# Top-k attention and highway layer on one core: a copy, two list rounds, warm matmuls and the end's products change places

## The chip, the cores and the metric

The kernel runs on one core of a Trainium2 chip. The core's engines work side by side, each on its own instructions in their order: TensorE (PE: matmuls and transposes; its weight loads are listed as PEld), VectorE (DVE), ScalarE (ACT), GpSimd (POOL), and SyncE (SP), which here issues DMAs. The metric is the device time of one execution in microseconds, as the median of several runs.

## The reference

For 8 batches of 8 heads, with 576 positions and head size 64, each query keeps the scores that are no smaller than its 32nd largest, takes a softmax over them and averages the values. The result goes, position by position, through a highway layer of width 512:

```python
scores = scale * np.matmul(q, k.transpose(0, 1, 3, 2))
kth = np.partition(scores, -top_k, axis=-1)[..., -top_k:-top_k + 1]   # top_k = 32
scores = np.where(scores >= kth, scores, -1000000000.0)
attn = softmax(scores)
x = np.matmul(attn, v)      # then to (4608, 512)
H = np.maximum(x @ w_h, 0.0)
T = 1.0 / (1.0 + np.exp(-(x @ w_t + b_t)))
return (T * H + (1.0 - T) * x)
```

(softmax is written out in the original.)

## The kernel before

**Tiling.** A group is 128 queries of one batch, for all 8 heads; queries are dealt to four groups per batch by their index modulo 4, and the 64 left over at the end of a batch share a group with those of the next batch. A group is worked through in pairs of tiles: one pair is two tiles of 128 queries by 576 keys. There are 144 pairs, numbered n, and the main loop (line 1016) makes one step for each.

**What happens to a pair.** `scores` (line 222) multiplies queries by keys on PE into a score bank in PSUM, of which there is one (`bigps`, bufs=1, line 99). `evac` (line 244) has ACT copy it with a Relu into SBUF, as z (zfirst for pair 0). `tree` (line 255) lets DVE take the maximum of the two halves of each row; for all pairs but the first two it reads one half from the score bank itself, so the bank is free again only when tree is done. `folds` (line 275) fold twice more on DVE, into hi, hh and h3 with widths 288, 144 and 72; POOL restores the smaller values by integer subtraction and addition (`minima`, line 298; pair 0's are done on DVE). `lists` (line 386) then draws sorted lists of eight from these with DVE's MAX8 and MATCH_REPLACE, and `lists_rest` merges them into the 32nd largest. ACT makes a penalty from it (pen), PE transposes score and penalty together, ACT takes the exponential (et), and `values` (line 1012, through `av`) multiplies it with the values; ACT copies this sum out as xs. When a group is complete, its rows are normed and go through the highway layer (`ffn_x`, `ffn_h`, `ffn_t`, `ffn_e`, `ffn_o`).

**The order of the work.** Instructions of PE, DVE, ACT and POOL are issued through a wrapper (`Pinned`, line 28) that keeps each engine's instructions in the order of the program, so the order written out by hand is the order on each engine, and line 38 is the line of nearly every instruction in the profile. The lists are Python generators, each of whose steps issues one instruction: `run(gens, rounds)` (line 411) takes so many steps of each list in turn. From step 3 on, unfinished lists are handed to `folds` as `fill`, which puts them between operations that depend on each other.

**The opening.** `turn_first` (line 144) transposes queries of the first tile: first for heads 0 and 1 (h0 = 0), then for the others (h0 = 1), and copies them into kq; on DVE in both cases. `turn` (line 175) transposes keys (kin 0, 1, 2, 3) and has ACT copy them. After its scores, step n puts WARM[n] matmuls without use on PE (`spin`, line 960), so that its clock stays granted: 9, 7 and 8 in steps 1, 2 and 3. In steps 0 and 1 `run(opening, 1)` takes one round of the pair's lists behind its folds; the rest follows in step 2, and what is left there is the fill of step 3.

**The end.** Behind the loop (from line 1114) the last pairs and the last two groups are written out by hand: gp, the last but one, and gl, the last. For gl, `final_norm` (DVE: a reciprocal and a product), `final_turn` (PE transpose, copy to xT on DVE, a half on POOL), `final_h` and `final_t` (PE products) are done in blocks of 128 columns as soon as heads are ready, so that little is left behind the last values. For gp, `ffn_gate` is a tanh on ACT, `ffn_e` a product on DVE over 512 columns (x <- t, x), `ffn_o` another one (d <- x, d) and an output transfer on SP's queue. `ffn_d(gl)` (d <- hps, xh) and `final_o` (two products on each half, and a transfer for each) end the program. `judge` turns the tests for a slower exact path into a flag.

Of the kernel before, what the change touches and what calls it, by code (L numbers as in the profile page):

```python
# [21 lines left out]
NZ = 3  # L22
NPEN = 3
IDLE = {11: 3, 10: 8, 9: 3, 3: 3, 2: 3}
WARM = {1: 9, 2: 7, 3: 8}


class Pinned:
# [42 lines left out]
class Ops:  # L71
# [72 lines left out]
    def turn_first(self, pr, h0, h1):  # L144


        nc, P = self.nc, self.P
        kqps = self.ztps.tile([P, 512], FP32, tag="zt", name="kqps")
        for hp in range(h0, h1):
            nc.tensor.transpose(  # L150
                kqps[:, hp * P : (hp + 1) * P],
                pr["qc"][:, 2 * hp : 2 * hp + 2, :].rearrange("p h d -> p (h d)"),
                self.ident[:],
            )
        nc.vector.tensor_copy(
            pr["kq"][:, 1, h0:h1, 0:P],
            kqps[:, h0 * P : h1 * P].rearrange("p (h q) -> p h q", q=P),
        )
# [644 lines left out]
def kernel(  # L803
# [10 lines left out]
    nc = tc.nc  # L814
# [60 lines left out]
    with ExitStack() as cm:  # L875
        ops = Ops(cm, tc, shared, exact=False)

        def load_weights():
            for src, dst in ((moe_w_h, wh), (moe_w_t, wt)):
                ops.nc.gpsimd.dma_start(  # L880
                    dst[:], src.rearrange("(g p) n -> p g n", p=P)
                )
            bt_bcast = bass.AP(
                tensor=moe_b_t.tensor, offset=moe_b_t.offset, ap=[[0, P], [1, dm]]
            )
            ops.nc.gpsimd.dma_start(bt[:], bt_bcast)
# [7 lines left out]
        def out_rows(g):  # L894
            if not g.rem:
                r0 = g.b * S + g.qt
                return [out[r0 : r0 + JP : J, :]]
            ends = [(g.b + i) * S for i in (0, 1)]
            return [out[r1 - R : r1, :] for r1 in ends]
# [48 lines left out]
        def have(n):  # L948
            return 0 <= n < NPR
# [10 lines left out]
        def spin(n, warm=None):  # L960
            if n and warm is None:
                warm = ops.fps.tile([P, 512], FP32, tag="fp", name="warm")
            for _ in range(n):
                ops.nc.tensor.matmul(
                    warm[:], idle[:, 0:P], idle[:], start=True, stop=True
                )
# [44 lines left out]
        late, fill, opening = [], [], []  # L1011
        def values(m):
            g, pi = pairs[m]
            ops.av(m, g, pi, preps[g.b]["vb"])

        while step <= NPR:
            n = step
            if have(n):
                ops.tree(n)
                if n < 2:  # L1020
                    ops.minima(n, ops.folds(n, *pairs[n], []))
                    opening += ops.lists(n, *pairs[n])
                    ops.run(opening, 1)
                elif n % 2:
                    nq = n // 2 + 1
                    ops.minima(nq, ops.folds(nq, *pairs[n - 1], fill))
                    fill = []
                if NHP <= n + 1 < 2 * NHP:
                    ops.turn(pr, "qin", n + 1 - NHP, None, 1)
                if n == NHP:  # L1030
                    ops.load(pr, "qin", 3, None, None, 1)
                if n == 2 * NHP:
                    ops.turn_rest(pr, 0, NHP, ("qrest",))
            if n == 5:
                load_weights()
            if have(n - 4):
                ops.mask(n - 4, *pairs[n - 4], tis=(0,))
            kind = fg = None
            nextg = None
            if ffn and (ffn[0][0] != "x" or n % 2):  # L1040
                kind, fg = ffn.pop(0)
                if kind == "t" and ffn and ffn[0][0] == "x":
                    nextg = ffn.pop(0)[1]
            if have(n - 5):
                spin(2 * (NPR - n < 12))
                values(n - 5)
            if have(n - 4):
                ops.mask(n - 4, *pairs[n - 4], tis=(1,))
            if have(n + 1):
                g, pi = pairs[n + 1]  # L1050
                spin(IDLE.get(NPR - n, 0))
                ops.scores(n + 1, g, pi, preps[g.b])
                ops.evac(n + 1)
                if n + 2 < NHP:
                    ops.turn(pr, "kin", n + 2, True)
            if n in WARM:
                spin(WARM[n], ops.ztps.tile([P, 512], FP32, tag="zt", name="warm"))
            if kind == "x":
                ops.ffn_x(fg)
            if kind == "h":  # L1060
                ops.ffn_h(fg)
                ops.ffn_r(fg)
                ops.ffn_d(fg)
            if nextg:
                ops.ffn_x(nextg)
            if kind == "t":
                ops.ffn_t(fg)
                if n < NPR - 1:
                    ops.ffn_e(fg)
                    ops.ffn_o(fg, *out_rows(fg))  # L1070
            if n == 3:
                ops.values_rest(pr)
                ops.values(pr, 0)
            if n == 4:
                ops.values(pr, 1)
            ended = False
            if have(n - 5):
                g, pi = pairs[n - 5]
                ended = pi == len(g.pairs) - 1 and (not g.rem or g.r0 > 0)
            if n % 2:  # L1080
                gens = ops.lists_rest(n // 2 - 1, *pairs[n - 3]) if have(n - 3) else []
                late = gens[2:]
                gens = gens[0:2]
                ops.run(gens)
                ops.run(late, 2)
            else:
                ops.run(late)
                if n == 2:
                    gens = opening
                else:  # L1090
                    gens = ops.lists(n - 2, *pairs[n - 2]) if have(n - 2) else []
                ops.run(gens, 2 * (n > 2))
                if ended:
                    ops.norm(pairs[n - 5][0])
                ops.run(gens, 3)
                if have(n + 1):
                    gens, fill = gens[0:2], gens[2:4]
                ops.run(gens)
            if have(n - 4):
                ops.trans(n - 4)  # L1100
            if ended and not pairs[n - 5][0].quick:
                ops.norm_heads(pairs[n - 5][0])
            for piece in pieces.pop(n, []):
                piece()
            if n % 2 == 0 and have(n - 3):
                g, pi = pairs[n - 3]
                if pi == len(g.pairs) - 1:
                    ops.settle(g)
            if ended:
                g = pairs[n - 5][0]  # L1110
                ffn += [("x", g), ("h", g), ("t", g)]
            step += 1
# [43 lines left out]
        part(1)  # L1156
        values(m + 1)
        ops.final_norm(gl, 2, 3)
        ops.ffn_gate(gp)
        ops.ffn_e(gp)  # L1160
        gl.ps = ops.fps.tile([P, 512], FP32, tag="fp", name="hps")
        ops.final_h(gl, 0, 2)
        values(m + 2)
        ops.final_turn(
            gl, 2, 3, ops.ztps.tile([P, 512], FP32, tag="zt", name="xtps")
        )
        ops.final_norm(gl, 3, 4)
        ops.final_t(gl, 0, 2)
        judge(banks[3])
        ops.final_turn(  # L1170
            gl, 3, 4, ops.ztps.tile([P, 512], FP32, tag="zt", name="xtps")
        )
        ops.ffn_o(gp, *out_rows(gp))
        ops.final_h(gl, 2, 3)
        ops.final_t(gl, 2, 3)
# [6 lines left out]
    with tc.If(taken > 0):  # L1182
        with tc.For_i(0, B, 1) as b:
            with ExitStack() as cm:
                ops = Ops(cm, tc, shared, exact=True)
# [17 lines left out]
                n = 0  # L1203
# [51 lines left out]
```

## Time and profile before

| | |
|---|---|
| median of 5 runs | 830.69 us (830.54 to 830.89) |
| profiled execution | 830.62 us |
| its span, first to last instruction | 828.9 us |
| mean granted TensorE clock | 0.989 |
| DVE busy | 814.1 us, 98% of the span |
| ACT busy | 760.4 us, 92% |
| POOL busy | 710.4 us, 86% |
| PE busy | 708.2 us, 85% |

All times in the profile are microseconds from the span's start. In a timeline row stand the start, the length, the engine, the line, the operation, what it writes and reads (`out<-in` by the program's names), its shape, and how often it follows itself; a bracket gives the idle time of the engine just before it, and what ended it. A row can stand for several equal instructions. Lengths of neighbours on one engine can overlap, so the cost of an instruction in a full queue is the distance from its start to the next one's.

### The profile page before, as it was taken

How to read it: one execution, taken by the hardware profiler on the slowest of the kernel's cores; microseconds unless marked ns; L12 is line 12 of the kernel's file. 1: busy time of each engine (PE TensorE's matmuls, PEld its weight loads, DVE VectorE, ACT ScalarE, POOL GpSimd, SP SyncE). 2: the span in 40 equal slices, each digit the busy share in tenths (PEclk: the TensorE clock that was granted, in tenths of full speed). 3: DMA queues.
4: the chain of work that ended last, by engine and by line, in shares of the span. 5: the costliest groups of instructions: out<-in, count | busy, mean ns of one | idle time of the engine just before them, and what ended most of it. 6: DMA issues, size and time to landing. Idle time of an engine off the chain costs nothing.

```text
span 828.9 us, 20198 instructions
## 1 busy us (share of the span) xinstructions
PE 708.2 (85%) x6582; PEld 490.0 (59%) x6635; DVE 814.1 (98%) x4173; ACT 760.4 (92%) x1522; POOL 710.4 (86%) x460
## 2 busy tenths in 40 slices
PE   8788888888888888888888898878988888899986
PEld 4565566565566556665566565656556655665654
DVE  5999999999999999999999999999999999999997
ACT  4899999899999999899999999989999999988985
POOL 5888888798889889978889988888888989887993
PEclk9999999999999999999999999999999999999999
DMA  8564233234254441433325342323413321211222
GB/s 183 136 109 84 65 90 75 59 68 88 40 101 85 78 90 30 75 71 65 90 53 92 70 93 61 64 53 71 110 32 65 52 40 40 40 35 26 45 39 56
DMA packets 105329, 58.40 MB, mean 70 GB/s; under 512 B 82304, under 2 KB 91904, under 8 KB 105216
## 3 DMA queue, kind: packets, MB, share of 16 engines
q1 hardware_dynamic: 93200, 37.47, 17.7%
q0 software_dynamic: 11200, 19.27, 16.4%
q8 instruction: 54, 0.88, 0.5%
q14 instruction: 59, 0.48, 0.2%
q10 hardware_dynamic: 816, 0.30, 0.1%
HBM read 30.67 MB, written 18.35 MB: 59 GB/s over the span
## 4 chain that ended last, share of the span: by engine, by line
DVE 94%; PE 3%; ACT 1%; POOL 1%; issue 0%; POOLq 0%; DVEq 0%
DVE w L38 53%; DVE m L38 20%; DVE hi L38 11%; DVE hh L38 6%; DVE h L38 3%; PE warm L38 1%; PE ps L38 1%; PE zt L38 1%; PE t L38 1%; DVE scales L38 0%; POOL hh L38 0%; ACT pen L38 0%; POOL hi L38 0%; ACT z L38 0%; ACT kq L38 0%
## 5 line engine op out<-in xcount | busy, mean ns | idle before, releaser
L38 PE MATMUL ps<-kq 64*128 64x64 f32 (+3 forms) x1280 | 202.9, 440 | 45.1 <-DVE hi L38 39.5
L38 ACT ACTIVATE pen<-z,m 128x576 bf16<-128x576 f32 x286 | 225.6, 790 | 1.2 <-DVE m L38 1.0
L38 PE MATMUL zt<-ident,z 128*128 128x128 f32 x1140 | 212.9, 280 | 2.0 <-ACT xT L38 2.0
L38 PE MATMUL zt<-nident,pen 128*128 128x128 bf16 x1148 | 205.5, 220 | 0.0
L38 ACT ACTIVATE z<-ps 128x1152 f32<-128x1152 f32 x143 | 161.8, 1131 | 43.6 <-PE ps L38 40.9
L38 POOL TENSOR_TENSOR hi<-z,hi 128x1152 int32<-128x1152 int32 (+1 forms) x72 | 188.2, 2613 | 11.2 <-DVE hh L38 5.6
L38 POOL TENSOR_TENSOR hi<-hi,z 128x1152 int32<-128x1152 int32 (+1 forms) x72 | 189.1, 2627 | 5.6
L38 PEld LDWEIGHTS ps<-kq 64*128 64x128 f32 (+1 forms) x1280 | 103.2, 177 | 140.9 <-issue 80.2
L38 PEld LDWEIGHTS zt<-ident,z 128*128 128x128 f32 x1140 | 161.3, 141 | 16.6 <-ACT xT L38 2.9
L38 ACT ACTIVATE et<-zt 128x512 bf16<-128x512 f32 x287 | 162.0, 601 | 5.6 <-PE zt L38 1.8
L38 POOL TENSOR_TENSOR hh<-hi,hh 128x576 int32<-128x576 int32 x71 | 104.5, 1471 | 70.9 <-DVE w L38 70.9
L38 PEld LDWEIGHTS <-pen 128*128 128x128 bf16 x1440 | 152.0, 106 | 16.1 <-ACT pen L38 10.7
L38 DVE MAX8 m<-w 128x8 f32<-128x168 f32 x576 | 158.8, 315 | 0.0
L38 PE MATMUL zr<-v,et 128*128 128x65 bf16 (+1 forms) x1590 | 98.1, 196 | 44.6 <-ACT et L38 37.3
L38 PEld LDWEIGHTS <-et 128*128 128x128 bf16 (+1 forms) x1600 | 69.1, 101 | 85.3 <-ACT et L38 82.4
L38 DVE MAX8 w<-hi 128x8 f32<-128x288 f32 x288 | 115.6, 440 | 0.0
L38 POOL TENSOR_TENSOR hh<-hh,hi 128x576 int32<-128x576 int32 x71 | 100.3, 1412 | 5.6
L38 DVE TENSOR_TENSOR hi<-ps,z 128x576 f32<-128x576 f32 x142 | 104.3, 734 | 0.5 <-ACT z L38 0.5
L38 DVE MAX8 w<-hh 128x8 f32<-128x72 f32 x576 | 96.4, 217 | 0.0
L38 DVE MATCH_REPLACE8 w<-m,w 128x168 f32<-128x168 f32 x288 | 88.6, 313 | 0.0
L38 PE MATMUL zr<-ident,z 128*128 128x128 f32 x284 | 67.3, 290 | 8.0 <-ACT xs L38 7.9
L38 ACT ACTIVATE x<-xs,scales 128x64 f32<-128x64 f32 x272 | 68.2, 336 | 0.0
(106 smaller groups left out, 1182.3 us busy)
## 6 DMA issues: line engine op xcount, KB each, us to landing
x<-d POOLq DMA_DIRECT2D x35, 256.0 KB, 3.8
vin<-in_v_dram SPq DMA_DIRECT2D x8, 1024.0 KB, 5.5
kin<-in_k_dram SPq DMA_DIRECT2D x63, 128.0 KB, 3.3
out_dram<-d SPq DMA_DIRECT2D x31, 256.0 KB, 2.3
out_dram<-t POOLq DMA_DIRECT2D x30, 256.0 KB, 4.2
qin<-in_q_dram SPq DMA_DIRECT2D x56, 128.0 KB, 3.0
qrest<-in_q_dram SPq DMA_DIRECT2D x8, 128.0 KB, 3.5
vrest<-in_v_dram SPq DMA_DIRECT2D x8, 128.0 KB, 3.1
```

The costliest lines, as they stand in the source:

```text
L38: return self._tc.keep_in_program_order(fn(*args, **kw))
```

## The change

Four edits. The copy of the other heads' queries of the first tile (h0 = 1) goes from DVE to ACT, where it stands behind the evacuation of pair 0 and ahead of the copy of kin 1. Pair 0's lists take three rounds in step 0 instead of one, so two MATCH_REPLACE and two MAX8 more stand ahead of pair 1's tree, and lists are finished in step 2, with nothing left as fill for step 3. Step 1 issues 5 warm matmuls instead of 9. At the end, gp's gate (ACT) goes behind the copy of the last values; gp's `ffn_e` (DVE) goes from behind the third block's norm to behind the last block's turn, just ahead of `ffn_o`; the last block's norm goes ahead of the third block's turn.

```diff
-WARM = {1: 9, 2: 7, 3: 8}
+WARM = {1: 5, 2: 7, 3: 8}
...
-        nc.vector.tensor_copy(
+        copy = nc.scalar.copy if h0 else nc.vector.tensor_copy
+        copy(
             pr["kq"][:, 1, h0:h1, 0:P],
             kqps[:, h0 * P : h1 * P].rearrange("p (h q) -> p h q", q=P),
         )
...
                     opening += ops.lists(n, *pairs[n])
-                    ops.run(opening, 1)
+                    ops.run(opening, 1 + 2 * (n == 0))
...
         values(m + 1)
         ops.final_norm(gl, 2, 3)
-        ops.ffn_gate(gp)
-        ops.ffn_e(gp)
         gl.ps = ops.fps.tile([P, 512], FP32, tag="fp", name="hps")
         ops.final_h(gl, 0, 2)
         values(m + 2)
+        ops.ffn_gate(gp)
+        ops.final_norm(gl, 3, 4)
         ops.final_turn(
             gl, 2, 3, ops.ztps.tile([P, 512], FP32, tag="zt", name="xtps")
         )
-        ops.final_norm(gl, 3, 4)
         ops.final_t(gl, 0, 2)
         judge(banks[3])
         ops.final_turn(
             gl, 3, 4, ops.ztps.tile([P, 512], FP32, tag="zt", name="xtps")
         )
+        ops.ffn_e(gp)
         ops.ffn_o(gp, *out_rows(gp))
```

## The prediction

> **What bounds the kernel now.** I read four views: busy time and the chain of waits on the page, then the timeline of the first 25 us and of the last 12 us, where the edits lie. From the page, engine shares and the engines of the chain that ended last:
>
> ```profile
> PE 708.2 (85%) x6582; PEld 490.0 (59%) x6635; DVE 814.1 (98%) x4173; ACT 760.4 (92%) x1522; POOL 710.4 (86%) x460
> ...
> DVE 94%; PE 3%; ACT 1%; POOL 1%; issue 0%; POOLq 0%; DVEq 0%
> ```
>
> VectorE (DVE) is the bound. From 22 to 800 us its waits add up to one of 0.4 us, so only its start, its stalls in the opening and its idle time at the end can change; the 780 us between are untouched. The timeline of the opening, all engines (start, length, engine, line, operation, in brackets the idle time before it and what ended it):
>
> ```profile
> 7.66 1.14 ACT L38 ACTIVATE zfirst<-ps 128x1152 f32<-128x1152 f32 x1 [1.28 <-PE ps L38]
> ...
> 8.12 0.56 DVE L38 COPY kq<-kqps 128x384 f32<-128x384 f32 x1 [2.01 <-PE kqps L38]
> ...
> 8.82 0.76 DVE L38 TENSOR_TENSOR hi<-zfirst 128x576 f32<-128x576 f32 x1
> ...
> 14.04 2.10 PE L38 MATMUL warm<-idle 128*128 128x512 bf16 x8
> ...
> 15.01 0.74 DVE L38 TENSOR_TENSOR hi<-ps,z 128x576 f32<-128x576 f32 x1
> ...
> 16.07 1.30 PE L38 MATMUL ps<-kq 64*128 64x512 f32 x8
> ...
> 17.42 1.13 ACT L38 ACTIVATE z<-ps 128x1152 f32<-128x1152 f32 x1 [2.15 <-PE ps L38]
> ...
> 18.58 0.76 DVE L38 TENSOR_TENSOR hi<-ps,z 128x576 f32<-128x576 f32 x1 [0.54 <-ACT z L38]
> ```
>
> Two things to see: the query copy on DVE is over (8.68) before zfirst is (8.80), and DVE starts its unbroken work at 8.82; and its only stall after that is 0.54 us before 18.58, for pair 3's scores. Those started on PE at 16.07, behind the warm matmuls, though their bank was free when tree(2) ended, 15.01 + 0.74 = 15.75. The timeline of DVE at the end:
>
> ```profile
> 818.68 0.17 DVE L38 RECIPROCAL scales<-xs 128x2 f32<-128x2 f32 x1 [0.42 <-ACT xs L38]
> 818.89 0.29 DVE L38 TENSOR_TENSOR x<-xs,scales 128x128 f32<-128x128 f32 x1
> 819.17 0.69 DVE L38 SCALAR_TENSOR_TENSOR x<-t,x 128x512 f32<-128x512 f32 x1
> 819.78 0.28 DVE L38 TENSOR_SCALAR xT<-xtps 128x128 bf16<-128x128 f32 x1
> 819.98 0.16 DVE L38 RECIPROCAL scales<-xs 128x2 f32<-128x2 f32 x1
> 820.17 0.29 DVE L38 TENSOR_TENSOR x<-xs,scales 128x128 f32<-128x128 f32 x1
> 820.95 0.29 DVE L38 TENSOR_SCALAR xT<-xtps 128x128 bf16<-128x128 f32 x1 [0.48 <-PE xtps L38]
> 821.32 0.69 DVE L38 SCALAR_TENSOR_TENSOR d<-x,d 128x512 f32<-128x512 f32 x1
> 821.93 0.68 DVE L38 SCALAR_TENSOR_TENSOR d<-hps,xh 128x512 f32<-128x512 f32 x1
> ```
>
> DVE idles 0.42 and 0.48 us here, but ffn_e (819.17) runs while PE and ScalarE (ACT) still produce the last block.
>
> **The opening, step by step.** All starts are of the execution before; times after are carried forward from them.
>
> Query copy to ACT. DVE gains nothing: 8.82 is set by zfirst. On ACT the copy stands behind zfirst and ahead of kin 1's copy, for which scores(1) waits. Price: the ACT copy of 128x384 at 23.72 let the next start at 24.08, 0.36 us (length 0.47). So scores(1) goes from 9.31 to 9.67, z(1) ends at 12.15, scores(2) starts at 12.68, z(2) ends at 15.15. This is hidden by DVE, which comes to tree(1) at 12.81 and tree(2) at 15.70 (next step). Without that cover it would cost its 0.36.
>
> The Trainium skill, "ScalarE: Activation LUTs", section "Rules for kernel authors", would have such plain elementwise work on VectorE, not ScalarE. The rows say otherwise here (0.56 us on DVE, 0.47 on ACT). By that page's 186 ns + 0.833 ns an element, less 93 ns of overlap, the copy would take about 0.41 us of ACT, an estimate; the sum stays the same.
>
> Two more rounds of pair 0's lists ahead of tree(1). A pair of MATCH_REPLACE is 0.41 us (14.32 to 14.73), a pair of MAX8 over 72 is 0.28 (15.66 to 15.94): 0.69 together. tree(1) goes from 12.12 to 12.81, tree(2) from 15.01 to 15.70, ending at 16.44. In step 1 one pair of MATCH_REPLACE is exchanged for another.
>
> Four fewer warm matmuls. Their spacing is 0.216 us (seven in 1.68, the last 0.38 long), so PE is free 0.86 earlier; with the 0.36 shift, at 16.07 - 0.86 + 0.36 = 15.57. But the score bank is single, and tree(2) reads it until 16.44. With 0.05 from DVE's end to PE's start (as at 821.24 to 821.29), scores(3) starts at 16.49, 0.42 later than before. From there PE and ACT take the same 2.51 (16.07 to 18.58): tree(3) at 19.00.
>
> What DVE does meanwhile. Step 2 now holds five pairs of MAX8 and two of MATCH_REPLACE: 15.70 + 0.65 + 5 x 0.28 + 2 x 0.40 = 18.55, and DVE waits 0.45 for z(3). Step 3 has no filler left, so hi, hh, h follow each other bare. A dependent pair costs 0.80 (8.82 to 9.62), hh 0.74 + 0.04, then 0.36 and 0.37 as now: 2.31 instead of 2.62 (18.58 to 21.20). DVE reaches the next step at 21.31, 0.11 later. The stall is mostly moved, and its filler was already filling bubbles. Opening: **+0.11**. Below: with no stall at all and the two bubbles of 0.12 still bare, -0.30. Above: the clock case below, +0.62 more. I take +0.11, since the single bank excludes the gain.
>
> SP's and POOL's orders are unchanged; POOL's first subtraction starts 0.69 later (15.25 instead of 14.56) and is done at 18.15, long before the list at 23.47 that reads it.
>
> **The end, step by step.** ACT: the last xs copy waits for PE's values until 819.28 with the gate ahead of it or not; the gate had ended at 819.15. So swapping them starts no copy earlier. The gate now starts 0.15 after it, at 819.43, and ends at 820.04, before anyone needs it; the flag copy behind it waits for PE at 820.34 anyway, and the tanh at 821.89 too.
>
> DVE: norm(2,3) as now (818.68, 818.89). The last reciprocal comes at 819.58 (xs done 819.55) instead of 819.98, its product at 819.79 to 820.08, xT of block 2 at 820.07. PE can turn block 3 after the judge's matmuls (820.15 + 0.19 = 820.34), against 820.61: xT of block 3 at 820.34 + 0.34 = 820.68 instead of 820.95, 0.27 earlier. PE's last products and tanh follow, and would be ready by 821.4.
>
> But now ffn_e (0.28 after xT as between 818.89 and 819.17) starts at 820.96, ffn_o needs its result, 0.69 + 0.04 later at 821.69, and ffn_d, behind both in DVE's queue, starts 0.61 later at 822.30 instead of 821.93. Everything behind it (final_o, the two output transfers, the end of the program) follows. ffn_e left a place where DVE had nothing else (it now waits 0.40 us there, until 819.58) and went into the path. ffn_o's own output transfer goes 0.37 later, still ahead of the last ones. End: **+0.37**. Below: block 3 turned at 820.23, xT followed after 0.20 (819.78 to 819.98): +0.15. Above: nothing earlier, and 0.37 and 0.80 of spacing: +0.80.
>
> **Sum.** +0.11 + 0.37 = +0.48 on the profiled execution's 830.62 (span 828.9 and 1.72 around it), which is 0.07 below the median of 830.69: I predict **831.1**. 0.2% is 1.66 us, about what a measurement of this kernel can tell from no change, so this counts as no change, leaning slow.
>
> **Rivals.** *The stalls really close.* If block 3's 0.27 reaches the end and the opening gives its 0.30, 830.62 - 0.57 = 830.05. For it: the gaps of 0.54, 0.42 and 0.48 are there. Against: ffn_e and ffn_o stand ahead of ffn_d, and the score bank is single.
>
> *A wash.* Small spacings of the two ends cancel: about 830.6. For it: the lower bounds, -0.30 and +0.15.
>
> *The clock dips once.* scores at 25.55 took 1.92 us instead of 1.30, after 2.20 us without work, at a granted clock of 0.68 (25 to 28 us). If scores(3) does that, +0.62: 831.7. Against: the gap before it is some 0.8 us, and scores(2) after 1.12 us took 1.30.
>
> The Trainium skill, "TensorE: Matmul & The Clock Gate", Part 1, puts the fall to half clock after an idle window of about 3.4 us. Here it came after a gap of 2.20, so the page's window is no safe bound for this trace; by it the term is 0, by the trace's row 0.62.
>
> *The clock stays down (slower).* If it is halved from scores(3) through scores(5), the 7 and 8 warm matmuls take 0.43 each (the first ones' spacing at 1.59, 2.02, 2.44) instead of 0.216, 1.5 and 1.7 us more, with 0.62 more for each scores. Scores(4) then starts near 22.5 and its z ends near 25.6, 0.2 after DVE needs it; z(5) ends near 32.1 instead of 30.8: 0.62 + 0.2 + 1.3 = 2.1, 833.2 in all. It decides as soon as scores(5) is over 1.3 us late. Against: the granted clock reads 1.00 in every slice up to 25 us.
>
> **How the numbers follow.** Forecast 0.68, closing stalls 0.06, wash 0.14, one dip 0.07, clock down 0.05. The range takes the wash and one dip with their spread, 830.3 to 832.0. Faster by over 0.2% would need under 829.0, which no case reaches: 0.02 for what I don't see. Slower 0.06, same 0.92.
>
> **What would show it.** Right: DVE's first hi still at about 8.8; tree(3) at about 19.0 with a wait of 0.4 to 0.5 for z; ffn_e at about 821.1 (820.96 and the opening's 0.11), directly ahead of ffn_o and ffn_d, with a new gap of 0.4 ahead of the last reciprocal. Wrong: tree(3) before 18.6, ffn_d no later than 821.93, a PE clock under 1.00 before 22 us, or DVE waits between 22 and 800 us.

## The result and the profile after

The changed kernel took 831.9 us in the median (24 runs, 830.77 to 833.13), the kernel before 830.79 (44 runs, 830.13 to 831.31): a ratio of 1.0014, with an interval of 1.0008 to 1.0019. That is 1.1 us more, within the 0.2% that counts as no change. A second comparison of the same two kernels gave 831.86 against 831.43, a ratio of 1.0006 (0.9997 to 1.0015). The predicted 831.1 was 0.48 over the profiled execution of before. What the sum left out is seen most plainly in the spread of the times, 2.4 us instead of 1.2.

The profiled execution of the changed kernel took 833.45 us (span 831.7): it is the slowest of its kind. Its page, engine shares and the engines of the chain that ended last:

```profile
PE 707.0 (85%) x6578; PEld 489.9 (59%) x6631; DVE 814.4 (98%) x4172; ACT 761.8 (92%) x1523; POOL 711.0 (85%) x460
...
DVE 95%; POOL 2%; PE 1%; issue 1%; ACT 0%; DVEq 0%; POOLq 0%
```

DVE is still the bound. The timeline of the opening, all engines:

```profile
7.66 1.13 ACT L38 ACTIVATE zfirst<-ps 128x1152 f32<-128x1152 f32 x1 [1.28 <-PE ps L38]
8.69 1.19 ACT L38 COPY kq<-kqps 128x384 f32<-128x384 f32 x3
8.82 0.76 DVE L38 TENSOR_TENSOR hi<-zfirst 128x576 f32<-128x576 f32 x1 [2.64 <-ACT zfirst L38]
...
14.42 1.24 PE L38 MATMUL warm<-idle 128*128 128x512 bf16 x4
15.69 0.73 DVE L38 TENSOR_TENSOR hi<-ps,z 128x576 f32<-128x576 f32 x1
...
16.57 1.30 PE L38 MATMUL ps<-kq 64*128 64x512 f32 x8 [0.90 <-DVE hi L38]
...
17.90 1.13 ACT L38 ACTIVATE z<-ps 128x1152 f32<-128x1152 f32 x1 [2.25 <-PE ps L38]
...
19.06 0.76 DVE L38 TENSOR_TENSOR hi<-ps,z 128x576 f32<-128x576 f32 x1 [0.48 <-ACT z L38]
```

DVE starts at 8.82 as before, though its copy is gone. (Of the five warm matmuls of step 1 the trace has four.) Scores 3 now wait for DVE's tree of pair 2 and no longer for warm matmuls, and the stall before the tree of pair 3 is 0.48 us, where it was 0.54. The next tree, of pair 4, comes 0.19 later. For before it reads

```profile
24.66 0.74 DVE L38 TENSOR_TENSOR hi<-ps,z 128x576 f32<-128x576 f32 x1
```

and for the changed kernel

```profile
24.85 0.74 DVE L38 TENSOR_TENSOR hi<-ps,z 128x576 f32<-128x576 f32 x1
```

The timeline of DVE at the end:

```profile
819.55 0.17 DVE L38 RECIPROCAL scales<-xs 128x2 f32<-128x2 f32 x1 [0.41 <-ACT xs L38]
...
820.46 0.17 DVE L38 RECIPROCAL scales<-xs 128x2 f32<-128x2 f32 x1 [0.42 <-ACT xs L38]
...
821.49 0.29 DVE L38 TENSOR_SCALAR xT<-xtps 128x128 bf16<-128x128 f32 x1 [0.33 <-PE xtps L38]
821.71 0.69 DVE L38 SCALAR_TENSOR_TENSOR x<-t,x 128x512 f32<-128x512 f32 x1
822.43 0.69 DVE L38 SCALAR_TENSOR_TENSOR d<-x,d 128x512 f32<-128x512 f32 x1
823.04 0.68 DVE L38 SCALAR_TENSOR_TENSOR d<-hps,xh 128x512 f32<-128x512 f32 x1
...
825.08 0.42 DVE L38 TENSOR_TENSOR o<-d,x 128x256 f32<-128x256 f32 x1
```

ffn_e (821.71) has left its old place, where DVE now waits 0.42 us, and stands in front of ffn_o and ffn_d. The last product of before is

```profile
823.97 0.43 DVE L38 TENSOR_TENSOR o<-d,x 128x256 f32<-128x256 f32 x1
```

From the start of the third block's reciprocal to the start of the last product it is 5.53 us (819.55 to 825.08), before 5.29 (818.68 to 823.97): 0.24 more.

So 0.19 and 0.24 lie where the order was changed. Two more differences stand between these two executions. One is in the group of the fold hh, which runs 71 times. In the groups of instructions (count, busy us, mean ns, idle time) it reads for before

```profile
L38 DVE TENSOR_TENSOR hh<-hi 128x576 f32<-128x576 f32 x71 | 56.3, 793 | 0.0
```

and for the changed kernel

```profile
L38 DVE TENSOR_TENSOR hh<-hi 128x576 f32<-128x576 f32 x71 | 57.0, 803 | 0.0
```

which is 0.7 us over the whole kernel, in an instruction that the change does not touch. The other is the landing of the last output transfer, the one that ACT issues. The transfers' issues of the last microseconds (KB each, us to landing) for before

```profile
out_dram<-d SPq DMA_DIRECT2D x1, 256.0 KB, 4.1
...
out_dram<-o ACTq DMA_DIRECT2D x1, 128.0 KB, 2.3
```

and for the changed kernel:

```profile
out_dram<-d SPq DMA_DIRECT2D x1, 256.0 KB, 2.9
...
out_dram<-o ACTq DMA_DIRECT2D x1, 128.0 KB, 4.2
```

The last one landed 1.9 us later after its issue. From the start of the last product to the end of the span it is 4.9 us for before (823.97 to 828.9) and 6.6 for the changed kernel (825.08 to 831.7), 1.7 more. With 0.19, 0.24 and the fold's 0.7 this is the whole 2.8 us between the two profiled spans. The experiments ask which of these four belongs to the change.

### The profile page after: what moved, and what is told of

Same layout as the page of the kernel before. It is cut to its first block, busy times and chain, and to the rows that moved or that the text cites. A ratio compares the mean times of both kernels' runs of the same rounds, so it can differ in the third digit from the quotient of the medians.

```text
span 831.7 us, 20189 instructions
## 1 busy us (share of the span) xinstructions
PE 707.0 (85%) x6578; PEld 489.9 (59%) x6631; DVE 814.4 (98%) x4172; ACT 761.8 (92%) x1523; POOL 711.0 (85%) x460
## 4 chain that ended last, share of the span: by engine, by line
DVE 95%; POOL 2%; PE 1%; issue 1%; ACT 0%; DVEq 0%; POOLq 0%
DVE w L38 53%; DVE m L38 20%; DVE hi L38 11%; DVE hh L38 6%; DVE h L38 3%; POOL hi L38 1%; POOL hh L38 1%; DVE scales L38 0%; PE warm L38 0%; PE ps L38 0%; DVE ok L38 0%; DVE d L38 0%; POOL t L38 0%; PE t L38 0%; DVE x L38 0%
```

## The experiments

Theory M is the prediction's: the order of DVE's queue at both ends makes the difference, and the rest is a matter of the single execution. Rival S: the edits of the opening leave the 770 us between slower. Rival T: the end's edits make the last landing late. One table of all profiles, to which the sections come back. "Tree 4" is the start of pair 4's tree after DVE's first fold; "end" is from the third block's reciprocal to the last product; "landing" and "fold hh" as shown above; "load" is how long after the last transfer's issue PE's second code load starts, explained below. The expectations use two other measures: for the fold the time from its start to the next instruction's start, and for the landing the time from the issue to the last packet, 0.4 to 0.8 us less than the listing's.

| kernel | tree 4, us | end, us | landing, us | load, us | fold hh, ns | median less before, us |
|---|---|---|---|---|---|---|
| before | 15.84 | 5.29 | 2.3 | 2.83 | 793 | |
| changed | 16.03 | 5.53 | 4.2 | 1.91 | 803 | 1.11 |
| changed, again | 16.04 | 5.54 | 4.0 | 1.80 | 801 | 0.43 |
| opening alone | 16.03 | 5.29 | 2.4 | 2.56 | 800 | 0.15 |
| end alone | 15.84 | 5.54 | 4.2 | 1.17 | 791 | 0.59 |
| norm alone | 15.84 | 5.09 | 2.2 | 2.01 | 794 | -0.19 |
| warm alone | 15.64 | 5.64 | 2.4 | 2.47 | 801 | -0.01 |
| copy alone | 16.22 | 5.80 | 2.2 | 1.76 | 802 | 0.65 |
| filler alone | 16.03 | 5.29 | 2.1 | 1.69 | 804 | 0.32 |
| warm and norm | 15.65 | 5.09 | 2.4 | 2.47 | 792 | -0.25 |
| end, six matmuls | 15.84 | 5.54 | 4.2 | 1.88 | 803 | 1.40 |
| changed, six matmuls | 16.04 | 5.53 | 2.1 | 1.39 | 803 | 0.91 |
| changed, PE waits | 16.05 | 5.54 | 2.5 | 3.17 | 796 | 0.90 |
| before, late output | 15.84 | 5.89 | 2.0 | 1.50 | 801 | 1.75 |

Each median is compared with before of its own session, which took 830.79 in the first and 831.17 to 831.43 us in the others. It comes with some 0.7 us of interval on either side (0.5 for the changed kernel's first), so single differences of 0.2 us are read from the trace and not from the times. In ten of these profiles it is 4.8 to 5.0 us from the start of the last product to the end of the span, in the four with a landing of 4.0 or more 6.4 to 6.6. So a late landing costs about 1.6 us of the time; these four executions took 832.74 to 833.54 us.

**The opening alone.** The three edits of the opening on the kernel before.

```diff
-WARM = {1: 9, 2: 7, 3: 8}
+WARM = {1: 5, 2: 7, 3: 8}
...
-        nc.vector.tensor_copy(
+        copy = nc.scalar.copy if h0 else nc.vector.tensor_copy
+        copy(
...
-                    ops.run(opening, 1)
+                    ops.run(opening, 1 + 2 * (n == 0))
```

> The three edits of the opening (copy on ACT, three rounds of pair 0's lists, 5 warm matmuls), with the end of before. The changed kernel's profile was later by 0.19 us at DVE's step 3 list, 0.24 over the end, and by 0.64 in a slow drift over the 770 us between; and its last output transfer landed 4.2 us after its issue instead of 2.3. Theory M (DVE's own queue, drift and landing are a matter of the single execution): 0.2 us over before, the tree of pair 3 at 19.06. Rival S (the opening leaves the steady stretch slower): 0.8 over, with the drift in the profile. Rival T (the end alone makes the last landing late): 0.2 over, landing 2.3.

Measured, without one execution of 3499 us: 831.32 against 831.17, ratio 1.0002 (0.9994 to 1.0011); tree 4 at 16.03, landing 2.4, end as before. The 0.19 of the trace is the opening's part. The fold was slow here too (800 ns), as rival S wants; whether that hangs on the edits had to wait for the other runs.

**The end alone.** The edits behind the loop as in the change, the opening of before.

> The end's edits alone, with the opening of before. Theory M: 0.25 us over before, from 3.25 us between the third block's reciprocal and ffn_d to 3.49. Rival S: the same 0.25, no drift. Rival T: 0.9 or more over before, the changed kernel's whole difference less the opening's 0.2, and times that scatter over 2 us as the changed kernel's do (before: 1.2).

Measured: 831.76 against 831.17, ratio 1.0009 (1.0000 to 1.0018), times from 831.41 to 833.09. The end is 5.54 us long, 0.25 more than before, as theory M says; the median is 0.59 over before, more than double that, but its interval reaches from 0.0 to 1.5 us. The last transfer was late again (4.2 us). Rival T has its first support: the old end landed in 2.2 to 2.4 us in the other three kernels of this round.

**The norm alone.** Of the end's edits only one: the last block's norm ahead of the third block's turn; gate and ffn_e stay.

```diff
+        ops.final_norm(gl, 3, 4)
         ops.final_turn(
             gl, 2, 3, ops.ztps.tile([P, 512], FP32, tag="zt", name="xtps")
         )
-        ops.final_norm(gl, 3, 4)
```

> Before, with one line of the end moved: the last block's norm ahead of the third block's turn; gate and ffn_e stay where they were. Theory M: the last reciprocal comes at 819.8, behind ffn_e, instead of 819.98, xT of the last block some 0.15 earlier and ffn_d with it: 0.15 to 0.25 under before. Rivals S and T say nothing else here; T adds that the scatter stays that of before.

Measured: 830.98 against 831.17, ratio 0.9996 (0.9987 to 1.0005). The end is 5.09 us, 0.20 less than before. So the earlier norm is worth 0.20, and it is the rest of the end's edits that costs, 0.24 + 0.20 = 0.44 us. That this is ffn_e's new place and not the gate's, which moved with it, is read from DVE's rows above, where ffn_e stands between the last xT and ffn_o; no run moves it alone.

**The warm matmuls alone.**

```diff
-WARM = {1: 9, 2: 7, 3: 8}
+WARM = {1: 5, 2: 7, 3: 8}
```

> Before, with 5 warm matmuls in step 1 instead of 9 and nothing else. Theory M: scores of pair 3 start when the tree of pair 2 ends (15.75) instead of 16.07, DVE's stall goes from 0.54 to 0.25, 0.27 under before. Rival: the shorter warming lowers the clock of scores 3, which then take up to 1.9 us, 0.35 over before. Rival S: a drift as in the changed kernel, if it is the warm matmuls that cause it.

Measured: 831.16 against 831.17, ratio 1.0000 (0.9992 to 1.0009). The timeline of the opening, PE and DVE:

```profile
14.04 1.24 PE L38 MATMUL warm<-idle 128*128 128x512 bf16 x5
15.02 0.74 DVE L38 TENSOR_TENSOR hi<-ps,z 128x576 f32<-128x576 f32 x1
15.90 1.30 PE L38 MATMUL ps<-kq 64*128 64x512 f32 x8 [0.62 <-DVE w L38]
...
18.40 0.76 DVE L38 TENSOR_TENSOR hi<-ps,z 128x576 f32<-128x576 f32 x1 [0.35 <-ACT z L38]
```

Scores 3 took 1.30 us, so the clock rival falls. The stall shrank to 0.35 and tree 4 came 0.20 earlier (15.64). The time did not show it: this execution had the slow fold (801 ns), and at the end ffn_e waited for something that the prediction had not seen, POOL's adding transfer into x. DVE's timeline there:

```profile
819.95 0.69 DVE L38 SCALAR_TENSOR_TENSOR x<-t,x 128x512 f32<-128x512 f32 x1 [0.36 <-DMA x<-d]
```

The transfer's last packet ended 0.51 us before ffn_e started (819.44). In the profile of before it ended 0.64 us ahead (818.53, ffn_e at 819.17): just in time.

**The end, with six matmuls behind PE's last product.** Two more kinds of records bear on the end: branches and loads of instructions (code loads). Once its products are issued, PE's sequencer goes to the program's last branch, on the flag. In the fourteen profiles the records show a code load of 16 KB 1.0 to 1.6 us after this branch starts, and a second one 2.0 to 2.9 us behind the end of the first. That both are PE's is read from these times alone. In the changed kernel's transfers, by queue (packets, MB, share), the window 827.4 to 828.5 us, holding that second load (827.45 to 828.48), reads

```profile
q8 instruction: 1, 0.02, 5.8%
q14 instruction: 2, 0.02, 5.7%
q10 hardware_dynamic: 1, 0.00, 0.5%
```

and 828.45 to 829.2 us, just behind it,

```profile
q10 hardware_dynamic: 9, 0.01, 6.2%
```

q10 carries ACT's transfer: 135 of its 144 packets are there by 826.96, the last eight rows and their completion from 828.46 on. In the end alone the last eight rows start at 827.63, where the load ends at 827.65; in this experiment at 828.52 and 828.54; in the changed kernel's second profile at 828.19 and 828.20. In the profiles that landed in time no rows of this transfer came so far behind the others. Theory T2: in the executions where they meet, these rows stand behind the load.

The packets of another transfer speak for it. In the profile of before, 120 of the 128 rows of gp's output (SP's transfer) are through at 823.70, and the last eight start at 824.64, where PE's first load ends at 824.65. All eight profiles with the old end (the late output below is one of them) have such eight rows, and they start at the load's end or up to 0.02 us before it. With the new end this transfer is issued later and shows no such gap; in the changed kernel's profile it lands in 2.9 us instead of 4.1.

Two things stay open. The load's start does not tell which execution lands late: in four profiles that landed in time it came 1.39 to 1.76 us after the issue, in the late ones 1.17 to 1.91. And in three of the four late ones its record starts 0.4 to 0.5 us after the other 120 rows were through, so that something not seen here held the eight rows, and perhaps the load too, before that.

To move the load away, PE was given work behind its last product.

```diff
         ops.final_t(gl, 3, 4)
+        spin(6, banks[3])
         ops.final_o(gl, out_rows(gl), (nc.sync, ops.nc.scalar))
```

> The end's edits alone, and behind PE's last product six matmuls without use (1.3 us). In the profile of the end's edits alone PE reached its last branch at 821.64; that branch loads code, at 822.67 and again 16 KB at 825.91 to 827.65, and the last packets of the last output transfer landed just behind that second load, 3.57 us after their issue at 824.74 (with the end of before 1.6 to 2.0, the load coming after them). Theory T2 (the second code load stands in front of these packets): with the branch 1.3 us later the packets land within 2.1 us, and the time is 0.25 us over before instead of 0.6. Rival (late landing for another reason that comes with the new order): landing stays at 3.6, the time at 0.6 or more.

Measured: 832.66 against 831.26, ratio 1.0012 (1.0003 to 1.0021); landing 4.2. The times fell in two heaps, 831.25 to 831.63 (five) and 832.66 to 833.54 (six). But the experiment missed its aim: PE began its last branch 3.06 us before ACT's issue, against 3.10 in the end alone. PE's sequencer does not wait for matmuls that it has only queued. So it tells nothing on T2 but one more late landing, and the two heaps.

**The changed kernel with the same six matmuls.** It failed in the same way, and so was the changed kernel again, in effect.

> The changed kernel with the same six matmuls behind PE's last product. Theory T2: its landing goes from 3.6 to about 2 us and its time from 1.1 over before to 0.4 to 0.6 over, and the scatter of the times from 2.3 to about 1.2 us. Rival: nothing changes, 1.1 over.

Measured: 832.17 against 831.26, ratio 1.0013 (1.0004 to 1.0022), 831.14 to 833.5. The profile fell on an execution that landed in 2.1 us, in which the load started when nearly all rows were through: the late landing is not there every time.

**The warm matmuls and the norm.** The two edits that the trace showed to gain, together.

> Before, with 5 warm matmuls in step 1 and the last block's norm ahead of the third block's turn. Theory M: 0.19 (the opening, as the profile with the warm matmuls alone had it) and 0.25 (the end) under before, 0.45 together. Rival S2 (with 5 warm matmuls GpSimd's products come some 0.02 us later against DVE, and the fold hh, which waits for them, takes 718 ns on the mean instead of 708 from start to next start, 0.6 us over the kernel): 0.1 us over to 0.1 under before, with the fold at 716 to 720 ns.

Measured: 831.01 against 831.26, ratio 0.9997 (0.9988 to 1.0006). Tree 4 at 15.65 and an end of 5.09 us: 0.39 less by the trace. The fold took 792 ns with 5 warm matmuls, so it does not hang on these: rival S2 falls. Of all versions this has the lowest median against its before, and its interval lies below that of the changed kernel's first comparison (1.0008 to 1.0019); whether it is faster than before, or than the norm alone, the times leave open.

**The copy alone.**

```diff
-        nc.vector.tensor_copy(
+        copy = nc.scalar.copy if h0 else nc.vector.tensor_copy
+        copy(
```

> Before, with only the copy of the other heads' queries on ACT; 9 warm matmuls, one list round. Theory M: the copy delays scores 1, 2 and, behind the 9 warm matmuls, scores 3 by 0.36 each, tree 3 comes at 18.94 and DVE's stall is 0.90: 0.36 over before; fold hh at 708 ns. Rival (the copy took something from DVE): no change or under before. Rival S2: fold hh as before, 708, since the warm matmuls are 9.

Measured: 831.91 against 831.26, ratio 1.0010 (1.0000 to 1.0019). The timeline, DVE's third tree:

```profile
18.35 0.76 DVE L38 TENSOR_TENSOR hi<-ps,z 128x576 f32<-128x576 f32 x1 [0.70 <-ACT z L38]
```

The stall is 0.70 and tree 4 comes 0.38 later, for an expected 0.36. The copy gains nothing on DVE and delays ACT's chain; in the whole change the longer filler hides that. The fold was slow with 9 warm matmuls (802 ns), which also speaks against S2. At the end ffn_e waited again, 0.51 us; the profile names ACT's last xs for it, which ffn_e does not read, and POOL's transfer had its last packet 0.51 us before (819.63, ffn_e at 820.14), as in the run above.

**The changed kernel, with PE held back.** A matmul of one column that reads gp's finished rows makes PE's sequencer wait.

```diff
         ops.final_t(gl, 3, 4)
+        ops.nc.tensor.matmul(
+            banks[3][0:1, 0:1], gp.d[:, 0:1], ones[:], start=True, stop=True
+        )
         ops.final_o(gl, out_rows(gl), (nc.sync, ops.nc.scalar))
```

> The changed kernel, and behind PE's last product one matmul of one column that reads gp's finished output rows, so PE's sequencer waits for ffn_o on DVE before it goes on to its last branch (the six matmuls without use did not hold it up: it reached the branch as early as without them). The branch then comes some 1.3 us later, at 823.7 on the changed kernel's clock, and its second code load near 828.5 or later, behind the last output transfer. Theory T2 (that load stands in front of the last transfer's packets in some executions): the last packets land within 2.4 us of their issue, the times lie in one heap of about 1.2 us width, 0.4 to 0.5 over before in the median. Rival: two heaps as in the changed kernel, 1.1 over.

Measured: 832.08 against 831.18, ratio 1.0011 (1.0002 to 1.0020), times from 831.21 to 832.4. PE's second load starts 3.17 us after the issue, and the landing is 2.5. None of 11 times lies over 832.4; of the changed kernel's 24 nine do, of its 11 in the second comparison two. So the upper heap seems to be gone, but these are few times. The median did not fall to 0.4 or 0.5 over before as expected; most times lie between 831.98 and 832.4. The profile fell on the fastest execution and so does not say what holds the others. PE's first load now falls beside the output transfers (eight rows of SP's last one start at 825.98, where it ends at 825.99), and PE comes to the end itself later; which of these it is stays open.

**Before, with the output later.** The load stays, the output moves: a sum into an unused tile on DVE.

```diff
         ops.final_h(gl, 3, 4)
+        scr = ops.fpool.tile([P, dm], FP32, tag="o", name="scr")
+        vec.tensor_tensor(scr[:], gl.x[:], gl.x[:], ALU.add)
         ops.ffn_d(gl)
```

> Before, with one sum over 512 columns into an unused tile added on DVE between ffn_o and ffn_d, 0.6 us; PE's branch stays where it is, the output transfers come 0.6 later. Theory M alone: 0.6 us over before. Theory T2: 0.6 over where the load misses the packets, and a second heap some 1.3 to 1.6 us above it where it meets them (the second load then starts 1.4 to 2.2 us after the last issue instead of 2.0 to 2.8), so more than 0.6 in the median and a scatter over 2 us.

Measured: 832.93 against 831.18, ratio 1.0018 (1.0009 to 1.0027). The end is 5.89 us, 0.60 more. The times lie in two heaps, 831.49 to 831.95 (five) and 832.93 to 833.5 (six), nothing in the 1.0 us between. The lower heap lies about 0.7 us over before, as M alone would have it, the upper one about 2.1. With six of eleven in the upper one, 0.6 us on DVE cost 1.75 in the median. This is T2's forecast, on the kernel before, by lateness alone: the order of the end's edits as such is not needed. The profile fell in the lower heap, with a landing of 2.0, so that the load is what holds the upper one here is inferred, not seen.

**The filler alone.**

```diff
-                    ops.run(opening, 1)
+                    ops.run(opening, 1 + 2 * (n == 0))
```

> Before, with only the three list rounds in step 0: the copy on DVE, 9 warm matmuls. Theory M: tree 2 starts 0.69 later, its end and not the warm matmuls sets scores 3, and DVE goes on to the tree of pair 4 as late as in the whole opening, 16.03 us after its first fold instead of 15.84: 0.19 over before. Rival (the filler saves something where the copy does not delay the scores): 15.84 or less.

Measured: 831.5 against 831.18, ratio 1.0002 (0.9993 to 1.0011); tree 4 at 16.03, exactly the whole opening's. So the filler alone sets the opening's 0.19, and copy and warm matmuls are covered by it.

**The changed kernel again.**

> The changed kernel again, profiled once more. Theory M with T2: everything that hangs on the order of work comes out as in its first profile (the tree of pair 4 16.03 us after DVE's first fold, 5.53 us from the third block's reciprocal to the last product), while the two things that vary between executions need not: the last packets land 1.4 to 2.1 or about 3.6 us after their issue, and the fold hh takes either 707 to 710 or 716 to 719 ns from start to start. Times 0.8 to 1.2 over before, scattered over 2 us. Rival: landing at 3.6 and the fold at 718 again, as properties of the kernel.

Measured: 831.86 against 831.43. The order's numbers repeat to 0.01 us (16.04 and 5.54). The landing was late again (4.0), the fold slow again (801 ns). Over all profiles the slow fold (800 ns or more) comes nine times in fourteen, with 5 warm matmuls and with 9, with either end; it is not the change's. The late landing came four times in five with the new end and no wait, and never in seven with the old end and its output in place.

## Why the prediction was right, point by point

The sign, the size of "no change" and the two places were right, and the measured 831.9 lies in the range of 830.3 to 832.0. That it does is partly luck: by the prediction's own terms, put right by the trace (0.43 instead of 0.48), the time would be 831.1, and the upper part of the range stood there for a dip of the clock that did not come. The 780 us between were untouched by the change, as predicted, but the fold makes them 0.7 us longer or shorter from one execution to the next.

*The query copy on ACT:* right. DVE's first fold did not move (8.82), and the copy's price alone was 0.38 us for a computed 0.36. The Trainium skill, "ScalarE: Activation LUTs", section "Rules for kernel authors", puts max, add, mul and the like on VectorE; it does not name a copy, to which the prediction carried it over. The copy of 128x384 took 0.47 us on ACT and 0.56 on DVE, but here neither length decided, only who waits behind it.

*The filler and the warm matmuls:* right in mechanism; the bank that tree 2 still reads set scores 3, and the stall moved to 0.48 for a computed 0.45. The opening's term was 0.11 and measured 0.19. PE started 0.15 after DVE's tree ended (16.42 to 16.57), where 0.05 was taken from the end of the kernel, and the bare folds took 0.02 more than their 2.31.

*The end:* right in mechanism, with ffn_e and ffn_o ahead of ffn_d. The term was 0.37 and measured 0.24, since ffn_e started 0.22 after the last xT where 0.28 was taken, and xT came 0.06 earlier than computed. (ffn_e stands at 821.71 in the profile, where 821.1 was named, since the slow fold had already made everything there 0.7 later.) The sum of both was 0.43 for a predicted 0.48.

*What failed:* the sentence "Everything behind it (final_o, the two output transfers, the end of the program) follows". It priced lateness at the end one to one. By the late-output run 0.6 us cost 1.75 in the median, with a gap of 1.0 us between the heaps, which fits last rows that fall behind a code load whose time PE sets and not DVE. In the changed kernel PE, with its last xT earlier against the output, even reached its branch earlier, 3.11 us before ACT's issue instead of 2.51, and the second load came 1.91 us after that issue instead of 2.83. A late landing costs 1.6 us where it comes, and the changed kernel's times look like a mixture: 13 of the 24 lie between 830.77 and 831.94, with a median of 831.25, which is 0.46 over before as the trace's 0.43 has it; the other 11 lie from 832.25 on. So the late landing is the main candidate for the 0.7 us between 0.43 and the first comparison's 1.1. It is not shown: no run takes the landing away and gets 0.4 in the median, and with PE held back no time lay over 832.4, but the median stayed at 0.90 over before.

*Rivals:* the stalls did not close (0.48 instead of 0.54, and 0.41, 0.42 and 0.33 at the end instead of 0.42 and 0.48). The clock neither dipped nor stayed down: scores 3 took 1.30 us after a gap of 0.90, with a granted clock of 1.00 up to 25 us. A wash is excluded by the first comparison, though not by the second alone. None of them was the mechanism that widened the times.

## What to carry to other kernels

A filler only gains if it stands where the engine would wait; moved ahead of the work that frees a buffer, it delays that work by its own length, and the wait comes back behind it. Where a queue has idle time while another engine finishes, an instruction put there is free; taken out and put behind the wait, it costs most of its length (here 0.44 of 0.69 us). At the end of a program, lateness need not be priced one to one: look in the trace at what the engines that have finished already load, and whether the last transfer stands behind it.

## What the runs showed of the hardware

*Code loads at the last branch.* PE's branch at the program's end lasted 3.4 to 4.2 us in the records, with a load of 16 KB inside it and a second one 0.8 to 1.5 us after its end, of 1.0 to 1.9 us each. The Trainium skill, "Runtime: NRT & Kernel Launch", section "Instruction fetch mechanics", says that a taken branch to a page outside the sequencer's window forces a DMA fetch before execution goes on; the first load agrees with that. The records add that eight rows of another engine's output came behind the rest and started where such a load ended, to 0.02 us, in thirteen of the fourteen profiles; in the four late ones they came 1.4 to 1.5 us behind.

*A sequencer that runs ahead.* Six queued matmuls did not hold PE's branch back (it began 3.06 us before the last issue, without them 3.10); a matmul that waits for DVE did (1.66 us before it instead of the changed kernel's 3.11).

*The fold and POOL.* The fold hh takes 0.66 us from start to start when POOL's product ends at most 0.1 us after its start, and beyond that about 1 us more for each 1 us that POOL ends later (0.68 us at 0.13 to 0.15, 0.78 at 0.23 to 0.25). One step of before

```profile
195.91 1.28 POOL L38 TENSOR_TENSOR t<-t,x 128x512 f32<-128x512 f32 x1
197.06 0.74 DVE L38 TENSOR_TENSOR hh<-hi 128x576 f32<-128x576 f32 x1
```

and the same step of the changed kernel:

```profile
196.25 1.28 POOL L38 TENSOR_TENSOR t<-t,x 128x512 f32<-128x512 f32 x1
197.36 0.78 DVE L38 TENSOR_TENSOR hh<-hi 128x576 f32<-128x576 f32 x1
```

The Trainium skill, "SBUF — State Buffer", section "SBUF: two separate sides", describes a port pair that VectorE and GpSimd take in turn, the loser blocked for the whole instruction, when VectorE's operation has two SBUF inputs and GpSimd's reads SBUF; the rows agree, as the fold lengthens with POOL's end. In the nine profiles with the slow fold POOL's two operations over 1152 columns took 2.644 us on the mean, in the other five 2.637, and the fold some 9 ns more, 0.6 us over the kernel. Which of the two drives the other, and what sets POOL's pace in an execution, was not found.

*A wait that comes and goes.* ffn_e in its old place waited 0.36 and 0.51 us in two of the profiles with the old end, by the transfer's packets both times for POOL's adding transfer, and not in the others. In its new place it comes too late to meet it.
